# Splitting the q and k loads of an attention and MLP-mixer kernel over two issuing engines

## The chip, the cores and the metric

The kernel runs on one core of one Trainium2 chip. The metric is device time in microseconds (us) of one execution, as the median of several. A run more than 1.5% above the fastest of the same kernel counts as slow; comparisons use fast runs only. All profiles shown below fell in fast runs, save two: one was a slow run, which is marked, and one ran only once.

Engine names: PE is the matrix engine (TensorE) and PEld its weight loads, DVE is VectorE, ACT is ScalarE, POOL is GpSimd, SP is SyncE. "SPq" and "ACTq" are DMA issues in SyncE's and in ScalarE's own instruction queue.

## The reference

Attention over 8 batches, 8 heads, 576 positions and 64 columns, with a causal mask and a decay bias built from `s`, and then an MLP mixer over tokens and over channels. Cut to what matters:

```python
cum    = np.cumsum(np.maximum(s, 0.0), axis=-1)
bias   = -(cum[:, :, :, None] - cum[:, :, None, :])
scores = q @ k.T / sqrt(64) + np.minimum(bias, 0.0)      # causal positions only
x      = (softmax(scores) @ v)                           # -> [8, 576, 512], float32
h      = np.maximum(x.T @ w_tok1, 0.0) @ w_tok2          # token MLP, 256 wide
u      = x + h.T
out    = u + np.maximum(u @ w_ch1, 0.0) @ w_ch2          # channel MLP, 1536 wide
```

## The kernel before

The kernel is a list of operations with a price each, and a small planner that simulates the engines and gives every operation an engine and a start. The program order is the order of these planned starts, so an engine's queue is fixed before the run. Nothing in an engine's queue passes what stands before it.

q and k of four heads (a "quad") share one tile. Each head is one DMA of 144 KB into 32 partitions, so heads 0 and 1 are the lower partition half and heads 2 and 3 the upper. All loads are issued by SyncE:

```python
def load_op(fn, key, us):                       # a load issued by SyncE, in order
    last[0] = P.op({"SP": (0.42, 0, fn)}, writes=key, prio=1, dma=us, after=last[0])

def load_quad(src, b, qd):
    f = Buf(r_qf)                               # one of 4 buffers, 128 x 1152 f32
    for g in range(4):
        load_op(lambda g=g: nc.sync.dma_start(
            out=f.t[32 * g : 32 * g + 32, :].rearrange("p (k n) -> p k n", n=R * D),
            in_=src[b, 4 * qd + g, :, :].rearrange("(k p r) d -> p k (r d)", p=32, r=R)),
            [(f, g)], S / R * 0.027 / 16)
    return f
# ... (cut) v: stage_v(b), five load_op of 256 or 128 KB, SyncE too
def hold():                                     # the gate: SyncE waits for the first channel weights
    last[0] = P.op({"SP": (0.6, 0, lambda: nc.sync.dma_start(out=gate[0:1, :], in_=wc2[0:1, 2, 0:16]))},
                   reads=[("wc2", 0)], writes=["gate"], prio=1, after=last[0])
# ... (cut) order of the loads
stage_qk(0, 0); stage_v(0); stage_qk(0, 1); load_tok(); stage_qk(1, 0)
# ... (cut) channel weights, by POOL
hold()
stage_v(1); stage_qk(1, 1)
for b in range(2, B):
    stage_qk(b, 0); stage_v(b); stage_qk(b, 1)
```

After a batch's attention come `tok(b)`, the token MLP, and `chan(b)`, the channel MLP. Between them u is transposed into `uTa` or `uTb`. For batches 0 and 1 PE transposes, and ScalarE or DVE copies the result out of PSUM (for batch 0 the planner gave all four copies to ScalarE). From batch 2 on a DMA issued by SyncE does it:

```python
if b >= 2:
    def trd(dst=dst, di=di, tc_=tc_):
        nc.sync.dma_start_transpose(out=uT.t[:, :, tc_ * 128 : tc_ * 128 + 128], in_=dst.t[:, di, :])
    # ... (cut) planned on SP
```

SyncE and ScalarE share eight completion semaphores. In the built program each of their DMAs takes the next of the eight in turn, and the engine that issues it first waits, in its own queue, until the DMA that used this semaphore before has landed.

Of the kernel before, what the change touches and what calls it, by code (L numbers as in the profile page):

```python
# [46 lines left out]
class Plan:  # L47
# [47 lines left out]
    def run(self, eps=0.03):  # L95
        ops = self.ops
        engines = ["PE", "ACT", "DVE", "POOL", "SP"]
        etime = {"PE": 0.0, "ACT": 2.1, "DVE": 2.5, "POOL": 2.0, "SP": 0.7}
        cands = {e: [] for e in engines}
        for o in ops:  # L100
            o.nd = len(o.deps)
            o.ready = 0.0
            o.done = False
            for d in o.deps:
                d.users.append(o)
        for o in ops:
            if o.nd == 0:
                for e in o.alts:
                    cands[e].append(o)
        dma_free = 0.0  # L110
        order = []

        def slot_time(o):
            t = 0.0
            want = {}
            for b in o.bufs:
                if b.slot is None:
                    r = b.ring
                    n = want.get(id(r), 0)
                    if b.ordered and (len(r.queue) <= n or r.queue[n] is not b):  # L120
                        return None
                    fr = sorted(r.free[i] for i in range(len(r.tiles)) if not r.busy[i])
                    if len(fr) <= n:
                        return None
                    t = max(t, fr[n])
                    want[id(r)] = n + 1
            return t

        left = len(ops)
        while left:  # L130
            best = None
            for e in engines:
                lst = []
                tmin = None
                for o in cands[e]:
                    st = slot_time(o)
                    if st is None:
                        continue
                    est = max(etime[e], o.ready, st)
                    lst.append((est, o))  # L140
                    if tmin is None or est < tmin:
                        tmin = est
                if tmin is None:
                    continue
                pick = None
                for est, o in lst:
                    if est <= tmin + eps:
                        key = (o.prio, o.idx) if e in ("PE", "SP", "POOL") else (o.prio, o.ready, o.idx)
                        if pick is None or key < pick[0]:
                            pick = (key, est, o)  # L150
                if best is None or pick[1] < best[1]:
                    best = (e, pick[1], pick[2])
            if best is None:
                stuck = [(e, len(c)) for e, c in cands.items()]
                raise RuntimeError(f"plan is stuck: {left} left, {stuck}")
            e, est, o = best
            occ, lat, fn = o.alts[e]
            for b in o.bufs:
                if b.slot is None:
                    r = b.ring  # L160
                    i = min((i for i in range(len(r.tiles)) if not r.busy[i]), key=lambda i: r.free[i])
                    b.slot = i
                    b.begin = est
                    r.uses.append(b)
                    r.busy[i] = True
                    if b.ordered:
                        r.queue.pop(0)
            etime[e] = est + occ
            if o.dma:
                s0 = max(est + 1.3, dma_free)  # L170
                dma_free = s0 + o.dma
                fin = dma_free + 0.9
            else:
                fin = est + lat
            o.start, o.fin, o.eng = est, fin, e
            for b in o.bufs:
                b.left -= 1
                b.end = max(b.end, fin)
                if b.left == 0:
                    b.ring.busy[b.slot] = False  # L180
                    b.ring.free[b.slot] = b.end
            for e2 in o.alts:
                cands[e2].remove(o)
            o.fn = fn
            order.append(o)
            for u in o.users:
                if u.after is o:
                    rdy = est + occ
                elif u.alts.keys() == {"PE"} and e == "PE":
                    rdy = est + occ  # L190
                elif e in u.alts and len(u.alts) == 1 and not o.dma:
                    rdy = est + occ
                else:
                    rdy = fin
                u.ready = max(u.ready, rdy)
                u.nd -= 1
                if u.nd == 0:
                    for e2 in u.alts:
                        cands[e2].append(u)
            left -= 1  # L200
        self.order = sorted(order, key=lambda o: (o.start, o.idx))
        self.length = max(o.fin for o in order)
        return self.order
# [131 lines left out]
def kernel(  # L335
# [12 lines left out]
    nc = tc.nc  # L348
# [67 lines left out]
    P = Plan()  # L416
    last = [None]

    def load_op(fn, key, us):

        last[0] = P.op({"SP": (0.42, 0, fn)}, writes=key, prio=1, dma=us, after=last[0])


    nc.vector.memset(zero[:, :], 0.0)  # L424
    make_identity(nc, ident)
# [19 lines left out]
    for i in range(1, 3):  # L445
        P.op({"DVE": (1.0, 1.2, lambda i=i: pads(nc.vector, i)), "POOL": (1.6, 1.8, lambda i=i: pads(nc.gpsimd, i))},
             writes=[("pad", i)], prio=40)
    P.op({"DVE": (0.6, 0.8, lambda: pads2(nc.vector)), "POOL": (1.0, 1.2, lambda: pads2(nc.gpsimd))},
         writes=["padw"], prio=41)
    P.op({"DVE": (0.3, 0.5, lambda: pads3(nc.vector, 1)), "POOL": (0.5, 0.7, lambda: pads3(nc.gpsimd, 1))},  # L450
         writes=["padv"], prio=42)
# [106 lines left out]

    def load_quad(src, b, qd):
        f = Buf(r_qf)  # L560
        for g in range(4):
            load_op(lambda g=g: nc.sync.dma_start(  # L562
                out=f.t[32 * g : 32 * g + 32, :].rearrange("p (k n) -> p k n", n=R * D),
                in_=src[b, 4 * qd + g, :, :].rearrange("(k p r) d -> p k (r d)", p=32, r=R)),
                [(f, g)], S / R * 0.027 / 16)
        return f
# [6 lines left out]
    def stage_qk(b, qd):  # L573
        for i, src in enumerate((k, q)):
            n = Buf(r_qn)
            qkn[(b, qd, i)] = n
            f = load_quad(src, b, qd)

            def cast(e, f=f, n=n):
                if e == 0:  # L580
                    nc.gpsimd.tensor_copy(out=n.t[:, :], in_=f.t[:, :])  # L581
                elif e == 1:
                    nc.vector.tensor_copy(out=n.t[:, :], in_=f.t[:, :])
                else:
                    nc.scalar.copy(out=n.t[:, :], in_=f.t[:, :])
            alts = {"POOL": (*c_pool(1152, 0.0010), lambda cast=cast: cast(0))}
            if b == 0 and (qd, i) != (1, 0):
                alts["DVE"] = (0.82, 1.04, lambda cast=cast: cast(1))
                alts["ACT"] = (*c_act(1152), lambda cast=cast: cast(2))
            castop[(b, qd, i)] = P.op(alts, reads=[(f, g) for g in range(4)], writes=[(n, 0)],  # L590
                                      prio=b * 10 + 4 * qd if b else 0)
            if b >= 2:
                square(n, [(n, 0)], (b * 2 + qd) * 2 + i)

    def stage_sq(b, qd):
        for i, src in enumerate((k, q)):
            f = load_quad(src, b, qd)
            square(f, [(f, g) for g in range(4)], (b * 2 + qd) * 2 + i)
# [377 lines left out]
```

## Time and profile before

| | before |
|---|---|
| median, four runs | 332.6 us (332.1 to 334.3) |
| span of the profiled run | 333.4 us |
| PE busy | 300.1 us (90%) |
| ScalarE busy | 168.6 us (51%) |

The profiled run took 335.3 us, a little more than any of the four that were timed, and each place in a trace is read from one run. Differences of 1 or 2 us between single traces are therefore not much to go by.

The first view is the page's part on the chain that ended last. It gives shares of the span, by what the chain passes through.

```profile
PE 42%; DMA 29%; SPq 11%; DVE 9%; issue 4%; POOL 2%; ACT 1%; POOLq 0%; ACTq 0%; DVEq 0%
```

DMA and SyncE's queue together hold 40% of the chain, about four fifths of it before 131 us (105.8 of 134.4 us). The next view is the table of busy time by stretch. Its columns are the stretch, its length, the busy us of each engine with its number of instructions, PE's granted clock (1 is full), the mean share of the DMA engines, and the GB/s they moved.

```profile
30.00:45.00 15.00, 13.84 (x153) 9.72 (x152) 9.86 (x25) 7.75 (x13) 5.33 (x8) 1.00 1.16 209
45.00:60.00 15.00, 14.84 (x111) 9.79 (x113) 4.69 (x13) 5.83 (x15) 7.38 (x7) 1.00 1.16 207
60.00:75.00 15.00, 11.34 (x133) 6.11 (x134) 10.71 (x20) 6.88 (x9) 9.08 (x9) 1.00 1.09 219
105.00:120.00 15.00, 14.80 (x123) 7.91 (x114) 10.94 (x22) 9.81 (x17) 8.94 (x9) 1.00 1.26 205
```

By their share the DMA engines are full in all four stretches, at 205 to 219 GB/s, and PE is busy for 11.3 to 14.8 us of each 15 us. Some of PE's work before 90 us is filler matmuls on zeros (29.4 us in all), whose results nothing uses.

ScalarE's timeline around batch 0's four `uTa` copies follows. The columns are start, duration, engine, line and operation. The bracket is the idle time before it and what ended it.

```profile
33.47 1.14 ACT L759 ACTIVATE h<-pmx 128x512 bf16<-128x512 f32 x2 [3.51 <-PE pmx L749]
37.67 2.26 ACT L803 COPY uTa<-pmx 128x512 bf16<-128x512 bf16 x4 [3.06 <-PE pmx L795]
40.75 1.94 ACT L647 ACTIVATE E<-psc 128x1024 bf16<-128x1024 f32 x2 [0.24 <-PE psc L628]
```

ScalarE waits for PE only, and batch 0's channel MLP starts on PE at 38.95 us. Last, SyncE's queue at the gate, and PE's one large gap after it:

```profile
40.51 0.62 SPq L723 DMA_DIRECT2D gate<-wc  x1
41.17 7.18 SPq L535 DMA_DIRECT2D vf<-in_v_dram  x5
67.21 2.17 SPq L562 DMA_DIRECT2D qkf<-in_k_dram  x4
```

```profile
134.19 1.44 PE L823 MATMUL pmx<-uTa,wc 128*128 128x512 bf16 x3 [6.54 <-DMA uTa<-ua]
```

SyncE may pass the gate at 40.5 us, and everything loaded after that starts there. The gap of 6.54 us is PE waiting for batch 2's transposes, which are DMAs in SyncE's queue.

### The profile page before, as it was taken

How to read it: one execution, taken by the hardware profiler on the slowest of the kernel's cores; microseconds unless marked ns; L12 is line 12 of the kernel's file. 1: busy time of each engine (PE TensorE's matmuls, PEld its weight loads, DVE VectorE, ACT ScalarE, POOL GpSimd, SP SyncE). 2: the span in 40 equal slices, each digit the busy share in tenths (PEclk: the TensorE clock that was granted, in tenths of full speed). 3: DMA queues.
4: the chain of work that ended last, by engine and by line, in shares of the span. 5: the costliest groups of instructions: out<-in, count | busy, mean ns of one | idle time of the engine just before them, and what ended most of it. 6: DMA issues, size and time to landing. Idle time of an engine off the chain costs nothing.

```text
span 333.4 us, 6640 instructions
## 1 busy us (share of the span) xinstructions
PE 300.1 (90%) x2557; PEld 167.4 (50%) x2593; DVE 181.4 (54%) x404; ACT 168.6 (51%) x269; POOL 86.8 (26%) x110
## 2 busy tenths in 40 slices
PE   6798999879799993899899998997999999999992
PEld 2356685435566441444466443543575445446640
DVE  4685642588678753116874583958561744350030
ACT  1364581347769455364397445973474418306500
POOL 3175225473737422051216120270000000000000
PEclk9599999999789999699999999999999999999997
DMA  8999999999999999898798279992400430042031
GB/s 153 202 195 208 208 215 203 183 251 223 227 208 187 203 202 186 209 227 195 152 246 163 58 176 233 180 176 73 102 2 0 90 134 2 34 95 79 3 96 69
DMA packets 109640, 50.45 MB, mean 151 GB/s; under 512 B 55904, under 2 KB 104416, under 8 KB 109600
## 3 DMA queue, kind: packets, MB, share of 16 engines
q1 hardware_dynamic: 106192, 46.17, 70.3%
q0 software_dynamic: 3408, 3.77, 6.7%
q8 instruction: 22, 0.36, 0.5%
q14 instruction: 18, 0.15, 0.2%
HBM read 40.71 MB, written 9.44 MB: 150 GB/s over the span
## 4 chain that ended last, share of the span: by engine, by line
PE 42%; DMA 29%; SPq 11%; DVE 9%; issue 4%; POOL 2%; ACT 1%; POOLq 0%; ACTq 0%; DVEq 0%
PE pmx L823 19%; PE pmx L841 15%; DMA qkf<-in_q_dram 12%; SPq L535 7%; DMA qkf<-in_k_dram 6%; SPq L562 4%; DMA wc<-in_moe_w_ch_dram 3%; DMA vf<-in_v_dram 3%; PE pmx L749 3%; DMA w<-in_moe_w_tok_dram 3%; PE pav L682 3%; DVE E L652 2%; PE psc L628 2%; POOL qkn L581 1%; DVE ub L777 1%
## 5 line engine op out<-in xcount | busy, mean ns | idle before, releaser
L823 PEld LDWEIGHTS <-wc 128*128 128x128 bf16 x624 | 59.6, 100 | 41.9 <-issue 12.1
L647 ACT ACTIVATE E<-psc 128x1024 bf16<-128x1024 f32 x64 | 62.1, 1020 | 31.1 <-PE psc L628 30.4
L823 PE MATMUL pmx<-uTb,wc 128*128 128x320 bf16 x384 | 58.1, 306 | 0.3 <-DMA uTb<-us 0.2
L581 POOL CAST qkn<-qkf 128x1152 bf16<-128x1152 f32 x29 | 34.1, 1183 | 87.4 <-DMA qkf<-in_k_dram 23.9
L841 PE MATMUL pmx<-wc,gb 128*128 128x512 bf16 x231 | 54.3, 379 | 0.4
L823 PE MATMUL pmx<-uTa,wc 128*128 128x512 bf16 (+1 forms) x236 | 46.4, 345 | 7.7 <-DMA uTa<-ua 6.5
L830 ACT ACTIVATE gb<-pmx 128x320 bf16<-128x320 f32 x74 | 32.1, 438 | 35.4 <-PE pmx L823 31.0
L544 POOL TENSOR_TENSOR vp<-vf,wT 128x512 bf16<-128x512 f32 (+1 forms) x35 | 37.0, 1078 | 35.8 <-PE pav L682 21.1
L841 PE MATMUL pmx<-wc,ga 128*128 128x512 bf16 x184 | 44.3, 379 | 0.9 <-issue 0.3
L569 ACT ACTIVATE junk<-qkn 128x1152 bf16<-128x1152 bf16 x24 | 27.9, 1162 | 24.1 <-POOL qkn L581 23.7
L652 DVE TENSOR_TENSOR E<-E,keep 128x512 bf16<-128x512 bf16 x64 | 32.5, 514 | 13.6 <-ACT E L647 13.4
L841 PEld LDWEIGHTS <-gb 128*128 128x128 bf16 x240 | 22.5, 98 | 25.2 <-issue 0.4
L682 PEld LDWEIGHTS <-E 128*128 128x128 bf16 x576 | 26.4, 98 | 15.5 <-DVE E L660 2.5
L830 ACT ACTIVATE ga<-pmx 128x512 bf16<-128x512 f32 (+1 forms) x43 | 22.0, 515 | 21.8 <-PE pmx L823 18.0
L694 DVE TENSOR_TENSOR x<-pav,rc 128x320 bf16<-128x320 f32 x60 | 29.4, 491 | 1.8
L682 PE MATMUL pav<-vp,E 128*128 128x65 bf16 x540 | 27.4, 195 | 3.2 <-DVE E L660 2.1
L927 PE MATMUL pmx<-zero 128*128 128x512 bf16 (+5 forms) x88 | 26.4, 431 | 2.7 <-DVE zero L424 1.2
L689 DVE RECIPROCAL rc<-pav 128x5 f32<-128x5 f32 x60 | 11.4, 189 | 30.2 <-PE pav L682 29.8
L841 PEld LDWEIGHTS <-ga 128*128 128x128 bf16 x192 | 17.6, 98 | 19.7 <-issue 1.1
L628 PE MATMUL psc<-qT,kT 32*128 32x256 bf16 (+2 forms) x640 | 23.8, 253 | 3.9 <-ACT E L647 3.2
L628 PEld LDWEIGHTS <-kT 32*128 32x128 bf16 x640 | 15.8, 93 | 16.1 <-issue 14.9
L852 DVE TENSOR_TENSOR of<-pmx,ua 128x512 f32<-128x512 f32 x16 | 10.9, 683 | 20.8 <-PE pmx L841 11.3
(81 smaller groups left out, 240.2 us busy)
## 6 DMA issues: line engine op xcount, KB each, us to landing
qkf<-in_k_dram SPq DMA_DIRECT2D x80, 144.0 KB, 4.8
qkf<-in_q_dram SPq DMA_DIRECT2D x80, 144.0 KB, 5.4
vf<-in_v_dram SPq DMA_DIRECT2D x32, 256.0 KB, 5.8
out_dram<-of SPq DMA_DIRECT2D x32, 256.0 KB, 2.5
wc<-in_moe_w_ch_dram POOLq DMA_DIRECT2D x8, 384.0 KB, 11.3
vf<-in_v_dram SPq DMA_DIRECT2D x8, 128.0 KB, 5.0
out_dram<-of SPq DMA_DIRECT2D x8, 128.0 KB, 2.4
w<-in_moe_w_tok_dram POOLq DMA_DIRECT2D x2, 256.0 KB, 8.8
```

What stands on the lines that cost most here:

```text
L544: eng.tensor_tensor(out=vp.t[p0 : p0 + n, c, :, 0:D], in0=vf.t[p0 : p0 + n, c, :, :], in1=wT[p0 : p0 + n, cw, b * H : b * H + H].unsqueeze ...
L569: P.op({"ACT": (1.2, 1.6, lambda: nc.scalar.activation(out=junk[:, :], in_=src.t[:, :], func=AF.Square, accum_out=sq[:, col : col + 1]))}, ...
L581: nc.gpsimd.tensor_copy(out=n.t[:, :], in_=f.t[:, :])
L628: nc.tensor.matmul(out=pss[g // 2].t[:, g % 2, c0 : c0 + z - a], lhsT=kT.t[rows, j0 : j0 + 128, e], rhs=qT.t[rows, a:z, e], start=(e == 0) ...
L647: nc.scalar.activation(out=E.t[:, :, gi * 512 : gi * 512 + 512], in_=ps.t[:, :, :], func=AF.Exp, scale=0.125)
L652: nc.vector.tensor_tensor(out=o, in0=o, in1=keep[:, :].unsqueeze(1).unsqueeze(1).to_broadcast([128, 2, 2, 128]), op=ALU.mult)
L682: nc.tensor.matmul(out=o[:, ic, 0 : D + 1], lhsT=E.t[:, hh, d0 : d0 + 128], rhs=vp.t[:, jc, h + hh, 0 : D + 1], start=(jc == j_lo), stop=( ...
L694: nc.vector.tensor_tensor(out=x.t[:, :, (h + hh) * D : (h + hh + 1) * D], in0=o[:, :, 0:D], in1=rc.t[:, :].unsqueeze(2).to_broadcast([128, ...
L823: nc.tensor.matmul(out=pm.t[:, 0 : e - a], lhsT=wc1[:, m, cc * 128 : cc * 128 + 128], rhs=uT.t[:, m, a:e], start=(m == 0), stop=(m == NMC ...
L830: lambda cc=cc, pm=pm, a=a, e=e: nc.scalar.activation(out=g.t[:, cc, a:e], in_=pm.t[:, 0 : e - a], func=AF.Relu),
L841: nc.tensor.matmul(out=pm.t[:, :], lhsT=g.t[:, cc, c * 128 : c * 128 + 128], rhs=wc2[:, cc, :], start=(cc == 0), stop=(cc == NCC - 1))
L927: f.fn = lambda t=r.tiles[slots[0]], n=n: nc.tensor.matmul(out=t[:, 0:n], lhsT=zero[:, 0:128], rhs=zero[:, 0:n], start=True, stop=True)
```

## The change

The intent: the loads of the two partition halves go out on two queues, so that both halves of the memory are written at once, and SyncE has half of its q and k issues (80 of 160) taken off. The heads are issued in the order 0, 2, 1, 3. Heads 0 and 1 stay on SyncE, heads 2 and 3 go to ScalarE. The planner learns that a second operation on a claimed buffer must wait until the buffer is free (`since`).

```diff
             for b in o.bufs:
-                if b.slot is None:
+                if b.slot is not None:
+                    t = max(t, b.since)
+                else:
# ... (cut)
                     b.slot = i
+                    b.since = r.free[i]
# ... (cut)
+    last2 = [None]
+
+    def load_op2(fn, key, us):
+
+        last2[0] = P.op({"ACT": (0.42, 0, fn)}, writes=key, prio=0, dma=us, after=last2[0])
# ... (cut)
-        for g in range(4):
-            load_op(lambda g=g: nc.sync.dma_start(
+        for g in (0, 2, 1, 3):
+            on, eng = (load_op, nc.sync) if g < 2 else (load_op2, nc.scalar)
+            on(lambda g=g, eng=eng: eng.dma_start(
```

## The prediction

> **What bounds the kernel now.** By the chain of waits, PE has 42% of the span, DMA transfers 29%, SyncE's queue 11%. The DMA part is almost all before 131 us: first loads and weights to 41 us, then v, q and k loads nearly back to back. After 134 us PE is dense to the end (13 to 15 us busy of each 15 us window). Before that, filler matmuls on zeros take 29.4 us, all before 90 us, and PE idles 6.5 us at 127.6 us, because the transposes of batch 2's u stand in SyncE's queue behind loads.
>
> In the loading phase the DMA share is 1.1 to 1.3 and the rate about 205 GB/s. A q/k load is 144 KB, issued in about 0.45 us, landing after about 5 us. In the built program these DMAs take eight completion semaphores in turn, so at most eight are in flight: 8 x 147 KB / 5 us = 236 GB/s, close to the four loads in 2.45 us that the timeline shows. SyncE pays for this limit by waiting, harmlessly.
>
> **What the change does.** 80 of 160 q/k issues leave SyncE (about 40 us of its queue) for ScalarE's in-order queue. No bytes change. The Trainium skill ("DMA: Bandwidth & Descriptors", Rules for kernel authors) says two transfers to disjoint partition halves are not worth issuing, as they share the same 16 DMA engines. The trace agrees so far: these engines are already full. I expect 0 to 10% more rate, worth 0 to 8 us.
>
> **What it costs.** ScalarE is 51% busy, so 80 issues of 0.45 us (36 us) would mostly fit. But each now waits, inside ScalarE's queue, for a buffer and for an earlier DMA on its semaphore, and the planner, which knows nothing of these semaphores, puts issues far ahead: most stand before an exp that in the trace ran 5 to 20 us earlier than the same load left SyncE.
>
> The worst place: the upper halves of quad (2,0) stand before the four uTa copies (37.7 us now), and wait for a chunk of batch 1's v and lower halves of quad (1,1). SyncE issues those only after the gate on the weights (40.5 us now); they land at about 52 to 54 us. So uTa copies, batch 0's channel MLP and quad (1,0)'s exps (40.8 us now) should slip 12 to 15 us, with PE idle for most of it. Batch 0's stores slip too, and hold later lower-half loads.
>
> **On the critical path.** Plus 12 to 15 us near 40 us; minus some 5 us of fillers and slack up to 90 us; minus 0 to 6 us at the 127 us gap, as SyncE's queue is shorter; plus 2 to 5 us of further ScalarE stalls to 150 us. After that PE's work is unchanged. Net about +9 us.
>
> Predicted 341 us, 80% between 331 and 352. Chances: faster by over 2% 0.08, within 2% 0.36, slower 0.56.
>
> **What will show it.** uTa copies starting at 50 to 54 us after a ScalarE queue wait on DMAs of v or q/k; PE idle over 8 us between 38 and 54 us; quad (1,0)'s first exp near 55 us; the loading rate within 10% of 205 GB/s; the gap at 127 us shorter; from batch 2's first channel matmul to the end about 200 us, as now.
>
> **What would make it wrong.** Two queues lifting the rate by 20% or more, so that the waits are short (then 320 to 326 us); the gate opening much earlier; or ScalarE stalls adding up at every quad (over 350 us).

## The result, and the profile after

| | before | after |
|---|---|---|
| median, four runs each | 332.6 us | 357.1 us (356.7 to 360.3) |
| ratio of fast runs | | 1.073, 95% interval 1.067 to 1.080 |
| span of the profiled run | 333.4 us | 355.4 us |
| PE busy | 300.1 us | 311.4 us |
| ScalarE busy | 168.6 us | 159.8 us |

Ratios here and below are the mean time of one kernel's fast runs over the mean of the other's of the same rounds, so they are not quite the ratios of the quoted medians.

The kernel is 7% slower. The prediction was 341 us with a range of 331 to 352, so the direction was right and the size was not.

The same views of the changed kernel follow, starting with the chain that ended last:

```profile
PE 53%; DMA 13%; DVE 5%; SPq 4%; ACT 2%; issue 2%; POOL 1%; ACTq 0%; DVEq 0%; POOLq 0%
```

The chain now passes less through DMA and more through PE, although the kernel is slower. Read alone this would mislead: the chain is followed back from the end, and PE's work on it is work that was delayed earlier. The table by stretch says when:

```profile
30.00:45.00 15.00, 10.73 (x88) 6.10 (x87) 8.75 (x17) 3.05 (x4) 4.42 (x7) 0.77 1.15 208
45.00:60.00 15.00, 4.06 (x35) 2.53 (x37) 2.46 (x5) 2.44 (x5) 8.61 (x8) 0.67 1.17 212
60.00:75.00 15.00, 14.84 (x144) 11.05 (x137) 7.38 (x13) 10.23 (x21) 6.87 (x6) 0.99 0.59 105
105.00:120.00 15.00, 9.51 (x116) 6.74 (x115) 11.03 (x27) 4.31 (x8) 3.91 (x4) 0.94 1.14 198
```

From 45 to 60 us PE has 4.06 us of work instead of 14.84, and ScalarE 2.44. The DMA rate in that stretch is 212 GB/s, as before. From 60 to 75 us it is the DMA engines that go half idle (105 GB/s), and from 105 to 120 us PE loses another 5 us. PE's granted clock is lower too in the idle stretch, 0.67 instead of 1.00; what part of the loss that makes was not separated. ScalarE's timeline shows the first loss:

```profile
38.73 0.60 ACT L769 ACTIVATE h<-pmx 128x512 bf16<-128x512 f32 x1 [6.58 <-PE pmx L759]
39.80 0.60 ACT L769 ACTIVATE h<-pmx 128x512 bf16<-128x512 f32 x1 [0.47 <-PE pmx L759]
39.88 13.17 ACTq L572 DMA_DIRECT2D qkf<-in_k_dram  x2
54.38 1.95 ACTq L572 DMA_DIRECT2D qkf<-in_q_dram  x2
56.43 2.05 ACT L813 COPY uTa<-pmx 128x512 bf16<-128x512 bf16 x4 [16.03 <-DMA qkf<-in_k_dram]
60.50 1.94 ACT L657 ACTIVATE E<-psc 128x1024 bf16<-128x1024 f32 x2 [0.53 <-PE psc L638]
```

The line with 13.17 us holds two issues of quad (2,0), the first quad of batch 2. The answer for the tile alone gives their own durations (shortest, median, longest, in ns) and starts:

```profile
L572 ACTq DMA_DIRECT2D qkf<-in_k_dram x2: 317/318/318, 39.9 to 52.7; - x2
```

Each issue takes 0.32 us. Between the end of the first (40.2 us) and the start of the second (52.7 us) ScalarE stands still for 12.5 us, with four `uTa` copies behind it. In the built program that second issue waits for the landing of a v chunk of batch 1, which SyncE issues only after the gate (41.2 us in this run). In the trace that chunk lands at 52.7 us, just before the issue. The Trainium skill ("DMA: Bandwidth & Descriptors", section "Anatomy of one DMA — SWDGE (gpsimd) path") notes that DMA engines don't wait on semaphores and that such a wait is spent on the issuing sequencer before dispatch. The page says it of GpSimd's path; here it shows for ScalarE's, with 12.5 us of standing still for a 0.32 us issue. PE's view of it, and its next large gap:

```profile
57.07 0.58 PE L805 MATMUL pmx<-ident,ua 128*128 128x128 bf16 x4 [10.94 <-ACT uTa L813]
57.64 1.91 PE L833 MATMUL pmx<-uTa,wc 128*128 128x256 bf16 x8
121.32 2.29 PE L833 MATMUL pmx<-uTb,wc 128*128 128x320 bf16 x8 [5.21 <-ACT gb L840]
```

The second gap has the same form, an issue on ScalarE between two evictions of batch 1's channel MLP:

```profile
113.20 0.32 ACTq L572 DMA_DIRECT2D qkf<-in_k_dram  x1
113.57 0.44 ACT L840 ACTIVATE gb<-pmx 128x320 bf16<-128x320 f32 x1 [3.84 <-DMA vf<-in_v_dram]
119.33 0.32 ACTq L572 DMA_DIRECT2D qkf<-in_k_dram  x1
119.69 1.16 ACT L579 ACTIVATE junk<-qkn 128x1152 bf16<-128x1152 bf16 x1 [5.69 <-DMA vf<-in_v_dram]
```

Counting the issues, these two are the k issues of quad (5,0). In the built program the second waits for the last v chunk of batch 4, and that lands in the trace at 119.3 us. The first waits for a k load of quad (4,1) that ScalarE had issued itself, which lands at 113.1 us; the v load named at 113.57 held the issues before it. SyncE's v loads were late at least in part because its queue stood, from 63 to 75.6 us, before the stores of batch 0, which the first stall had delayed:

```profile
41.21 0.61 SPq L733 DMA_DIRECT2D gate<-wc  x1
56.97 6.19 SPq L544 DMA_DIRECT2D vf<-in_v_dram  x5
75.64 2.94 SPq L867 DMA_DIRECT2D out_dram<-of  x2
78.68 0.92 SPq L572 DMA_DIRECT2D qkf<-in_k_dram  x2
```

Before, quad (2,1)'s k loads left SyncE at 67.2 us; now they leave at 78.7 us.

A table of PE's first matmul of each stage shows where the 22.0 us between the two spans came from. The column of `same_plan_sp` is explained with that experiment.

| stage begins on PE, us | before | after | after less before | `same_plan_sp` |
|---|---|---|---|---|
| channel MLP, batch 0 | 38.95 | 57.64 | 18.7 | 45.80 |
| channel MLP, batch 1 | 90.27 | 106.29 | 16.0 | 93.37 |
| token MLP, batch 2 | 107.79 | 131.29 | 23.5 | 108.92 |
| channel MLP, batch 2 | 134.19 | 155.83 | 21.6 | 136.59 |
| token MLP, batch 3 | 147.83 | 173.44 | 25.6 | 149.96 |
| channel MLP, batch 4 | 202.34 | 227.94 | 25.6 | 204.47 |
| channel MLP, batch 7 | 300.60 | 322.57 | 22.0 | 299.13 |

### The profile page after: what moved, and what is told of

The parts are those of the page before. It is cut to its first block, busy times and chain, and to the rows that moved or that the text cites. A ratio compares the mean times of both kernels' runs of the same rounds, so it can differ in the third digit from the quotient of the medians.

```text
span 355.4 us, 6731 instructions
## 1 busy us (share of the span) xinstructions
PE 311.4 (88%) x2611; PEld 169.8 (48%) x2611; DVE 196.1 (55%) x422; ACT 159.8 (45%) x251; POOL 86.9 (24%) x110
## 4 chain that ended last, share of the span: by engine, by line
PE 53%; DMA 13%; DVE 5%; SPq 4%; ACT 2%; issue 2%; POOL 1%; ACTq 0%; DVEq 0%; POOLq 0%
PE pmx L851 21%; PE pmx L833 21%; DMA vf<-in_v_dram 10%; DMA qkf<-in_k_dram 3%; PE pmx L759 3%; PE pav L692 3%; SPq L544 3%; PE psc L638 3%; PE pmx L780 2%; ACT junk L579 1%; DVE E L662 1%; DVE E L670 1%; SPq L572 1%; ACT E L657 1%; DVE kT L617 1%
## 5 line engine op out<-in xcount | busy, mean ns | idle before, releaser
L851 PE MATMUL pmx<-wc,gb 128*128 128x512 bf16 x240 | 56.8, 388 | 0.0
L833 PE MATMUL pmx<-uTa,wc 128*128 128x512 bf16 (+1 forms) x240 | 47.5, 348 | 4.4 <-ACT ga L840 3.8
L851 PE MATMUL pmx<-wc,ga 128*128 128x512 bf16 x192 | 45.2, 379 | 0.1
L662 DVE TENSOR_TENSOR E<-E,keep 128x512 bf16<-128x512 bf16 x64 | 37.2, 584 | 14.2 <-ACT E L657 13.8
L840 ACT ACTIVATE gb<-pmx 128x320 bf16<-128x320 f32 x64 | 27.7, 437 | 29.8 <-PE pmx L833 22.0
L937 PE MATMUL pmx<-zero 128*128 128x512 bf16 (+5 forms) x114 | 32.2, 427 | 1.2 <-DVE zero L433 1.2
L840 ACT ACTIVATE ga<-pmx 128x512 bf16<-128x512 f32 (+1 forms) x39 | 19.4, 504 | 20.3 <-PE pmx L833 19.7
L842 DVE TENSOR_SCALAR ga<-pmx 128x512 bf16<-128x512 f32 (+1 forms) x21 | 12.3, 595 | 18.7 <-PE pmx L833 18.7
```

Of the source, the lines that this page charges most:

```text
L662: nc.vector.tensor_tensor(out=o, in0=o, in1=keep[:, :].unsqueeze(1).unsqueeze(1).to_broadcast([128, 2, 2, 128]), op=ALU.mult)
L833: nc.tensor.matmul(out=pm.t[:, 0 : e - a], lhsT=wc1[:, m, cc * 128 : cc * 128 + 128], rhs=uT.t[:, m, a:e], start=(m == 0), stop=(m == NMC ...
L840: lambda cc=cc, pm=pm, a=a, e=e: nc.scalar.activation(out=g.t[:, cc, a:e], in_=pm.t[:, 0 : e - a], func=AF.Relu),
L851: nc.tensor.matmul(out=pm.t[:, :], lhsT=g.t[:, cc, c * 128 : c * 128 + 128], rhs=wc2[:, cc, :], start=(cc == 0), stop=(cc == NCC - 1))
L937: f.fn = lambda t=r.tiles[slots[0]], n=n: nc.tensor.matmul(out=t[:, 0:n], lhsT=zero[:, 0:128], rhs=zero[:, 0:n], start=True, stop=True)
```

## The experiments

Fourteen kernels ran, on the chip, each beside runs of the kernel before on the same chip (medians 333.0 to 333.7 us). All results were correct except that of the rate test.

Two kinds of experiment have to be told apart. In `same_plan_sp`, `late_20` and `late_all` the built programs give every engine the same other instructions in the same order as in the changed kernel, and so does `act_0213` beside `before_0213`; only DMA issues differ. In `split_late`, `split_early`, `quad20_sp`, `quad50_sp`, `quad2050_sp` and `after_nohold` the edit changes what the planner is given, and it plans anew. ScalarE's count of instructions on the page shows it: 251 in the changed kernel, and 257, 263, 254, 252 and 256 in the first five of these. (`after_nohold` has 251 again, but another order.) The total times of these six mix the edit with another plan. In `split_early`, `quad20_sp`, `quad50_sp` and `quad2050_sp` the programs first differ only after batch 0's channel MLP has begun on PE, so what they show of the first stall is not touched by this.

### 1. What the queues themselves do

The kernel's body is replaced by bare loads of the same shapes, in seven phases with a barrier between them. Core of the edit:

```diff
+        for i in range(N):                     # 2: SyncE, halves in turn
+            for g in (0, 2, 1, 3):
+                quarter(nc.sync, i, g)
+        barrier()
+        for i in range(N):                     # 3: as the change: lower SyncE, upper ScalarE
+            for g in (0, 2, 1, 3):
+                quarter(nc.sync if g < 2 else nc.scalar, i, g)
```

> Load rates alone, wrong result on purpose: seven phases of loads, each closed by a barrier. 1 SyncE alone, heads in order; 2 SyncE alone, halves in turn; 3 lower halves SyncE, upper halves ScalarE, as the change; 4 both queues, but each queue gets both halves; 5 v alone; 6 v on SyncE beside upper halves on ScalarE; 7 the same all on SyncE. My theory (ScalarE stalls, the rate does not matter): phase 3 within 10% of phase 1, about 240 GB/s; 6 within 10% of 7. Rival A (two queues get in each other's way): phase 3 or 6 slower than 1 or 7 by over 10%. The intent of the change: phase 3 faster than 1 by 20% or more, and than 4.

The stretches of the first four phases, in the order: SyncE with heads in order; SyncE with halves in turn; the change's split; two queues that each take both halves. The last number is GB/s.

```profile
5.00:45.00 40.00, 2.31 (x15) 0.00 (x0) 1.00 1.22 219
51.00:86.00 35.00, 2.31 (x15) 0.00 (x0) 1.00 1.21 242
92.00:128.00 36.00, 2.15 (x14) 0.00 (x0) 1.00 1.22 234
135.00:172.00 37.00, 2.15 (x14) 0.00 (x0) 1.00 1.22 223
```

A tile of 590 KB took 2.68, 2.44, 2.55 and 2.65 us in these phases. The test ran once. Two queues, split as in the change, are 5% faster than one queue with the heads in order, and no faster than one queue with the halves in turn. The Trainium skill ("DMA: Bandwidth & Descriptors", section "Issuing engines are not separate DMA queues") says that DMAs from different engines share the same 16 DMA engines, and that issuing from several only saves sequencer time. This run agrees. What it did show is that the order of the heads on one queue is worth 10% (219 to 242 GB/s), and that at a DMA share of 1.22 and 1.21: a full share does not mean that no more bytes could be moved. Loading v beside split q and k (210 GB/s) and all of it on SyncE (206) hardly differ.

### 2. The plan without the queue

The change's planner and order, but the upper halves' DMAs issued by SyncE:

```diff
-            on, eng = (load_op, nc.sync) if g < 2 else (load_op2, nc.scalar)
+            on, eng = (load_op, nc.sync) if g < 2 else (load_op2, nc.sync)
```

> The planner's order of the changed kernel kept, but the upper halves issued by SyncE; ScalarE issues no DMA. My theory (ScalarE's queue is held up by its DMA issues): back to 325 to 341 us, uTa copies of batch 0 before 43 us. Rival B (the planner's new order of the other instructions, its extra fillers included, is what costs): stays above 350 us. Rival A (two queues slow the loads) also expects about 333 us here, and is told apart by the rates.

332.8 us (331.8 to 333.7), ratio 0.998 (0.993 to 1.003). The new plan alone costs nothing at the end, so practically all of the 24.5 us between the medians comes with ScalarE as the issuer. But the table above shows that batch 0's channel MLP starts at 45.8 us in it, 6.9 us later than before. So of the 18.7 us at that point in the changed kernel, 6.9 us also appear without ScalarE issuing anything, and 11.8 us come with its issues. ScalarE's copies show the same 12 us (44.5 us here, 56.4 in the changed kernel), and here they wait for PE:

```profile
44.48 2.27 ACT L813 COPY uTa<-pmx 128x512 bf16<-128x512 bf16 x4 [3.94 <-PE pmx L805]
```

Most of the 6.9 us is there before the stalled issue: the token MLP's first `h` runs at 38.9 us here and at 38.7 in the changed kernel, against 33.5 before. In this kernel the 6.9 us are almost gone by batch 2's token MLP (1.1 us). The kernel says nothing on halves in turn, as its plan often parts the halves of a quad: the upper ones of quad (2,0) leave SyncE at 34.3 to 36.2 us, before the gate, and the lower ones at 54.8 to 56.7.

### 3. Only the later batches split, only the earlier batches split

```diff
-            on, eng = (load_op, nc.sync) if g < 2 else (load_op2, nc.scalar)
+            on, eng = (load_op, nc.sync) if g < 2 or b < 3 else (load_op2, nc.scalar)    # split_late
+            on, eng = (load_op, nc.sync) if g < 2 or b > 2 else (load_op2, nc.scalar)    # split_early
```

> Only batches 3 to 7 split, batches 0 to 2 all on SyncE, so the ScalarE wait at 40 us cannot occur. My theory: uTa copies of batch 0 at 37 to 40 us, as before; later ScalarE stalls remain; 336 to 346 us. Rival A (slower loads) and rival B (new order): most of the loss stays, 348 us or more, since most loads are still split.

335.1 us (331.3 to 335.6), ratio 1.003 (0.995 to 1.011): even less loss than expected, just below my range. This plan differs from the start.

> Only batches 0 to 2 split over the two engines; batches 3 to 7 all on SyncE. Theory: the early stall is whole, the channel MLP of batch 0 starts at 55 to 60 us, and the total is 348 to 358 us, against 357 with all split and 335 with only the later ones split. Rival (each split batch costs its share, some 3 us): 338 to 345.

343.2 us (342.5 to 345.0), ratio 1.029 (1.022 to 1.035). My theory expected 348 to 358 and missed; the rival's range of 338 to 345 held it. The rival's reason does not hold, though: the early stall is there in full (batch 0's channel MLP at 56.7 us). But with the later batches on SyncE about half of it is won back, and batch 2's channel MLP starts only 7.9 us later than before, against 21.6 in the changed kernel. In excess of the before of their own rounds, splitting late costs about 0.3%, early 2.9%, both 7.3%. The costs don't add, though part of this may lie in the three plans.

### 4. The gate

```diff
-    hold()
     stage_v(1)
```

> The changed kernel without the gate that holds SyncE's loads of batch 1 until the first wc2 weights are there. My theory: the upper halves of quad (2,0) no longer wait for gated loads, the wait before batch 0's uTa copies falls from 16 us to under 6 us, and the time to 335 to 348 us (the weights land some us later, which costs part). If the gate plays no part in the stall: 352 us or more.

355.6 us (354.8 to 358.4), ratio 1.068. This missed. ScalarE's waits in this run show why:

```profile
ACT E L657 <- DMA qkf<-in_q_dram: 14.7, 2, 8.3
ACT h L769 <- DMA vf<-in_v_dram: 13.7, 1, 13.7
```

Without the gate SyncE's v loads run beside the weights and land late, and ScalarE stands just as long, only before other instructions (13.7 us before the token MLP's `h`). The gate sets where ScalarE waits. It is not needed for the wait, as far as this other plan can show.

### 5. Four issues, then four others

Quad (2,0)'s upper halves, four of the 80 issues, go back to SyncE; then quad (5,0)'s alone; then both.

```diff
-            on, eng = (load_op, nc.sync) if g < 2 else (load_op2, nc.scalar)
+            on, eng = (load_op, nc.sync) if g < 2 or (b, qd) == (2, 0) else (load_op2, nc.scalar)
# quad50_sp:   (b, qd) == (5, 0)
# quad2050_sp: (b, qd) in ((2, 0), (5, 0))
```

> The whole change, but the upper halves of quad (2,0) alone are issued by SyncE (4 of the 80 issues). Theory: the batch 0 channel MLP starts at 38 to 47 us, total 333 to 346 us; what remains over before is the later stalls (in the changed kernel 7.5 us were added at batch 2's token MLP and 4.0 at batch 3's). Rival (many small stalls or queue disturbance): total over 350.

336.2 us (333.8 to 340.0), ratio 1.005 (0.998 to 1.011). The median is that of all four runs; of the three fast ones it is 335.3. The theory held. Its profiled run was the slow one (span 338.2 us), so only its order of events is read. ScalarE's copies come when PE has transposed, as before:

```profile
45.58 2.26 ACT L813 COPY uTa<-pmx 128x512 bf16<-128x512 bf16 x4 [4.22 <-PE pmx L805]
```

> The whole change, but the upper halves of quad (5,0) alone are issued by SyncE. In the changed kernel its second k issue on ScalarE left only at 119.3 us, after a wait of 5.7 us on the landing of a v load of SyncE's, between two evictions of batch 1's channel MLP. Theory (the early stall makes SyncE late, and a second stall follows where a later issue on ScalarE stands behind one of SyncE's late v loads): the early stall stays whole (batch 0's channel MLP at 55 to 60 us), batch 2's token MLP comes 4 us or more earlier than in the changed kernel (131.3), total 346 to 353 us. Rival (the wait just moves to the next ScalarE issue, no one quad matters): total over 354.

350.4 us (347.6 to 353.9; one run was slow, the fast ones have 349.0), ratio 1.055 (1.048 to 1.063), in the theory's range. The early stall is whole (57.9 us), and batch 2's token MLP starts at 124.1 us instead of 131.3.

> The whole change, but the upper halves of quads (2,0) and (5,0) are issued by SyncE (8 of 80 issues). With (2,0) alone on SyncE the time was 336.2 us, with (5,0) alone 350.4. If the second stall is a thing of its own: 328 to 333 us. If it only follows from the early stall and SyncE's lateness, which is gone once (2,0) is on SyncE: the same as with (2,0) alone, 334 to 338 us; I expect this.

332.1 us (330.1 to 332.7), ratio 0.995 (0.989 to 1.001). I expected 334 to 338 and missed. This points to a second stall that is partly a thing of its own, not only an echo of the first, but does not show it: the interval of `quad20_sp` (0.998 to 1.011) overlaps with this one, and the plans differ. With these 8 of the 80 issues back on SyncE, and planned anew, the change takes as long as the kernel before; in this plan the other 72 issues on ScalarE cost nothing against before that these runs can see.

### 6. The same issues on ScalarE, at a later place

The plan stays, and after planning the upper halves' issues are moved back in program order, to 8 us (planned) before their first reader. In `late_20` this is done for quad (2,0) alone, in `late_all` for every quad.

```diff
     order = P.run()
# ... (cut) `upper` lists the batch and the operation of every upper half's issue
+    for b, o in upper:
+        need = min(u.start for u in o.users if u.eng != "ACT" or not u.dma)
+        if b == 2 and o.start < 35.0:          # late_20; `if True` in late_all
+            o.start = max(o.start, need - 8.0)
+    order.sort(key=lambda o: (o.start, o.idx))
```

> The whole change, and the plan as it is, but the four ScalarE issues of quad (2,0) are moved in the program from just before the four uTa copies of batch 0 to about 8 us (planned time) before the casts that read them; nothing else moves and the loads keep their queue. Theory (ScalarE's in-order queue stands behind DMAs that are not done, and that one place makes most of the loss): uTa copies within 8 us of before (38 to 46 us instead of 57), total 334 to 346 us. Rival 1 (two DMA queues disturb each other, or the copies are late for another reason): copies stay at 52 us or later, total over 352. Rival 2 (the loss is many small stalls, the early one is absorbed by slack): copies early, but the total over 350.

348.6 us (347.0 to 350.9), ratio 1.044. This missed my range by 2.5 us. The copies came early (45.1 us), as the theory says, but ScalarE then stood in the next place:

```profile
60.38 2.85 ACTq L573 DMA_DIRECT2D qkf<-in_q_dram  x2
68.11 1.86 ACTq L573 DMA_DIRECT2D qkf<-in_k_dram  x2
73.35 1.16 ACT L582 ACTIVATE junk<-qkn 128x1152 bf16<-128x1152 bf16 x1 [13.85 <-DMA qkf<-in_q_dram]
```

Moving one wait of an in-order queue does not remove it if the following issues wait as well. A moved issue also takes another of the eight semaphores, and so can wait for another DMA; these two kernels do not tell that apart from the later place.

> The whole change, every upper-half issue on ScalarE, but each moved in the program to no earlier than 8 us (planned) before its first reader. Theory: little of the stall is left, total 330 to 342 us, ScalarE's longest wait on a DMA under 8 us. Rival (ScalarE as an issuer costs by itself, wherever the issues stand, or two queues collide): over 348 us.

337.9 us (337.8 to 339.0), ratio 1.013 (1.008 to 1.019). In range, although ScalarE's longest wait on a DMA was 9.3 us and not under 8. Most of the loss depends on where the issues stand.

### 7. Another plan, only the issuer changed

The kernel before, with heads in the order 0, 2, 1, 3, planned for SyncE alone; then the same plan with the upper halves' DMAs given to ScalarE at the same planned times.

```diff
-        for g in range(4):
-            load_op(lambda g=g: nc.sync.dma_start(
+        for g in (0, 2, 1, 3):                                # before_0213: this line alone
+            eng = nc.sync if g < 2 else nc.scalar             # act_0213 only
+            load_op(lambda g=g, eng=eng: eng.dma_start(       # act_0213 only
```

> The kernel before with its four heads issued in the order 0, 2, 1, 3, all by SyncE. In the rate test the two partition halves taken in turn on one queue took 2.44 us for a tile of 590 KB, in order 2.68 us. If the loading phase is bound by that rate: 3 to 6 us faster, 327 to 330 us. If it is bound by waits of SyncE for buffers and other DMAs (weights, v), as I now rather think: 331 to 334 us, the same.

324.6 us (323.0 to 325.0), ratio 0.973 (0.969 to 0.978). Faster than I had expected of either reading. Up to 75 us the four issues of a k or q load mostly take 1.9 to 2.2 us of SyncE's queue instead of 2.0 to 2.6 (two take 3.4, one of them below), the gate opens earlier, and later loads come earlier (compare the same lines of before):

```profile
37.98 0.62 SPq L723 DMA_DIRECT2D gate<-wc  x1
38.65 6.93 SPq L535 DMA_DIRECT2D vf<-in_v_dram  x5
62.77 3.40 SPq L562 DMA_DIRECT2D qkf<-in_k_dram  x4
```

```profile
60.00:75.00 15.00, 14.94 (x185) 8.02 (x184) 11.98 (x28) 9.17 (x13) 9.48 (x10) 1.00 0.99 250
```

From 60 to 75 us it moves 250 GB/s where before had 219, at a lower DMA share (0.99 against 1.09).

> The kernel before with heads in the order 0, 2, 1, 3, the plan made for SyncE alone (that version took 324.6 us), and the upper halves' issues then given to ScalarE at the very same planned times: every engine's other instructions stand in the same order, and only the issuing engine of 80 DMAs differs. Theory (an issue on ScalarE holds its computations while it waits for a DMA, wherever the planner thinks the issue cheap): uTa copies of batch 0 still near 39 us, as the issues stand behind them here, but ScalarE waits of some us each on DMAs before exps and evictions at batches 1 to 5, total 329 to 342 us. Rival 1 (only the planner's new order in the changed kernel is bad, the issuer does not matter): 321 to 328 us. Rival 2 (two queues load faster): under 321.

344.5 us (343.2 to 345.6), ratio 1.035 (1.029 to 1.040), against 0.973 for the same plan on SyncE. The two ran in different rounds; by the ratios to before (1.035 over 0.973) the issuing engine, with all that follows from it, costs about 6%, some 20 us. That is a little over my range, and against both rivals. ScalarE's queue shows the toll, issue by issue, between instructions that follow one another without such gaps in `before_0213`:

```profile
54.84 0.32 ACTq L563 DMA_DIRECT2D qkf<-in_k_dram  x1
55.26 1.02 ACT L648 ACTIVATE E<-psc 128x1024 bf16<-128x1024 f32 x1 [5.78 <-DMA qkf<-in_q_dram]
57.49 0.32 ACTq L563 DMA_DIRECT2D qkf<-in_k_dram  x1
57.85 0.38 ACT L831 ACTIVATE ga<-pmx 128x256 bf16<-128x256 f32 x1 [1.57 <-DMA qkf<-in_k_dram]
```

Here no planned order of the change is involved and the `uTa` copies are not behind an issue (they start at 42.5 us, when PE has transposed), and still the loss is there.

### 8. A version that beats both

Batch 2's u is transposed by PE instead of by SyncE's DMA, alone and with the order of experiment 7:

```diff
-            if b >= 2:
+            if b >= 3:
```

> The kernel before, but batch 2's u is transposed by PE, as batches 0 and 1 are, not by a DMA of SyncE's. In the kernel before PE idles 6.5 us at 127.6 us for that DMA. If that gap is on the critical path: PE gets some 1 to 2 us more work and evictions, the gap goes, total 327 to 330 us. If what follows is bound by the loads of batch 3 anyway: 332 to 335 us.

329.5 us (327.4 to 330.7), ratio 0.988 (0.983 to 0.993). In range; some of the gap of 6.54 us was on the critical path.

> Both of the last two edits. If each removes its own limit: 322 to 328 us. If they are one limit or none: 329 to 334 us.

318.7 us (317.5 to 321.6), ratio 0.959 (0.954 to 0.965), below even my lower range of 322 to 328. The two edits remove different limits, as together they gain about what the two gain alone (4.1% against 2.7% and 1.2%), and the result takes 4% less time than before and 11% less than the change.

## Why the prediction was right or wrong

**Right: the mechanism and the place.** "The upper halves of quad (2,0) stand before the four uTa copies (37.7 us now), and wait for a chunk of batch 1's v and lower halves of quad (1,1)." ScalarE stood 12.5 us at that issue, and taking those four issues away (`quad20_sp`) brought 357.1 us down to 336.2. ScalarE's queue wait, the idle PE, and the delayed stores that hold later loads all appeared.

**Right: the bytes.** "I expect 0 to 10% more rate." The loading stretches of the changed kernel from 30 to 60 us run at 208 and 212 GB/s, before at 209 and 207. The rate test agrees (7% over the heads in order). The Trainium skill's rule that the prediction cited, on two transfers to disjoint partition halves, held in so far as a second queue added nothing to halves in turn on one (2.55 us a tile against 2.44).

**A little under: the first stall.** "Should slip 12 to 15 us." Batch 0's channel MLP slipped 18.7 us, and the copies came at 56.4 us, not at 50 to 54. ScalarE's waits made 11.8 of it by comparison with `same_plan_sp`; 6.9 us were there with SyncE issuing in the new plan as well. I had read the new plan for what stands before what, and had no term for its delay of the start.

**Wrong: what is won back, and what is added.** The failed step is the sum "minus some 5 us of fillers and slack up to 90 us; minus 0 to 6 us at the 127 us gap, as SyncE's queue is shorter; plus 2 to 5 us of further ScalarE stalls to 150 us". By the table of stages the terms measured:

| term | predicted | measured |
|---|---|---|
| first stall, to batch 0's channel MLP | +12 to +15 | +18.7 |
| won back, to batch 1's channel MLP | −5 | −2.7 |
| further stalls, to batch 2's token MLP | +2 to +5 in all | +7.5 |
| the gap before batch 2's channel MLP | 0 to −6 | −1.9 |
| further stalls, to batch 3's token MLP | (in the +2 to +5) | +4.0 |
| rest, to the end | 0 | −3.6 |
| sum | +9 | +22.0 |

The last column adds up to the difference of the two spans. The further stalls were 11.5 us, more than twice the top of my range, and they lie partly in the one place that the trace shows, quad (5,0): without its four issues on ScalarE, in a kernel planned anew, batch 2's token MLP came 7.2 us earlier and the whole 7 us. I had treated the early stall as a delay that later slack eats. `split_early` suggests that this is right when the later loads are on SyncE (about half was won back, with another plan). In the changed kernel the stall makes SyncE late, SyncE's late v loads then hold the next issues on ScalarE, and what was to be slack becomes a second stall.

**What stays open.** The full size of this interplay is not settled. Early split alone costs 2.9%, late split alone 0.3%, both 7.3%, and the three plans differ, so that part of this may be the plan. Quad (5,0) explains about 7 us of the 13 or so that are more than the sum; the rest was not pinned to an issue. Nor is it shown how the completion semaphores would behave if they were not shared, as their number and sharing can't be changed in these kernels. That issues on ScalarE wait for DMAs of SyncE's is read from the built program and from the landings and releasers in the trace. What the lower granted clock of PE adds was not tested either.

**What the prediction missed outright.** The change holds a useful part: taking the halves in turn. On SyncE alone it gives 2.7% (`before_0213`). I had thought about rate only as a matter of two queues.

## What to carry to other kernels

An engine that computes should issue a DMA only where the issue can't wait, because, as here, everything behind it in its queue waits too. The price of an issue was not its 0.32 us but the wait for whatever had to land first, and that can be a DMA of another engine's. Before moving issues, list what each waits for and what stands behind it, and don't count on slack to eat a stall in a system where late computing makes late loads. When a change combines an order and an engine, try the order alone: here it was the part worth having.

## What the Trainium skill lacked or had wrong

- "DMA: Bandwidth & Descriptors", section "Issuing engines are not separate DMA queues": it names as the one effect of several issuing engines a saving of sequencer time, and has nothing on the price when one of them also computes. Here that price was some 20 us for 80 issues of one plan (ratio to before 1.035 instead of 0.973), and in the change practically all of the loss (357.1 us with 80 issues on ScalarE, 332.8 with none in the same plan; 332.1 with 8 of them moved back, in another plan).
- No page that I read has the case in which two issuing engines take completion semaphores from one small pool, so that an issue on one waits for a landing on the other. Here one 0.32 us issue stood 12.5 us.
- "DMA: Bandwidth & Descriptors", section "Rules for kernel authors", row on two transfers to disjoint partition halves: it advises against them, and two queues did not help here against the same order on one (2.55 us a tile against 2.44). But it has nothing on the order in which 32-partition transfers go out on one queue, where the data makes them necessary. Halves in turn moved 242 GB/s, heads in order 219, and the whole kernel went from 333.0 to 324.6 us.
- "SBUF — State Buffer", section "Can I just issue two DMAs to hit both halves?": it gives 6% for two concurrent DMAs on the two halves over a single one. With many such DMAs in flight on one queue, putting the halves in turn gave 10% over the heads in order here, which is another comparison. The page's map of partitions to ports (section "Door 1: The DMA port swizzle") would fit this, but no run here separates ports from other reasons.
